# A new written-out order for the first 28 steps of a fused windowed-attention and feed-forward kernel

## The chip, the cores and the metric

The kernel runs on one core of a Trainium2 chip. The metric is device time in microseconds (us) for one execution. A run of the kernel before is given as the median of three. One further execution was profiled, and every trace number comes from that one.

## What is computed

The reference has two parts. The first is attention over 8 batches, 8 heads, 576 tokens and a head size of 64. A query sees at most 32 keys: in the first four heads the 32 latest tokens, in the other four every fourth token of the latest 128. The second part is a feed-forward network on the 4608 tokens with 512 columns, over 2048 hidden columns.

```
scores = scale * q @ k.T;  scores = where(mask, scores, -1e9)
attn   = exp(scores - max(scores));  attn = attn / (sum(attn) + 1e-9)
x      = attn @ v                      # reshaped to 4608 x 512
h      = x @ w_in
out    = (h * clip(h + 3, 0, 6) / 6) @ w_out
```

## The kernel before

**Tiles.** Attention is cut into 48 pieces, called trios here after the name in the code; a trio is 192 token rows of four heads. Tokens for the feed-forward part are cut into 12 chunks of 384, hidden columns into 16 blocks of 128. The matmuls of the feed-forward part keep full precision by three products: high part by high part, low by high, high by low. So each x and each weight is split into two tiles first.

**Steps.** A step is one chunk by one block of hidden columns: a first product G (12 matmuls, L486 to L488), a ReLU on ScalarE (L494), a gate on VectorE (L497), a split into two parts (ScalarE L501, VectorE L505), and a second product H (9 matmuls, L536 to L538). Chunks 0 and 1 take turns in the first 32 steps. The first chunk needs trios 0 to 4, the second trios 2 to 9.

**The written order.** The first 28 steps, the first 12 trios, the split of all weights and all their loads are ordered by hand in one string, `ORDER`, of 588 names. Each engine keeps the order in which its own names stand there. TensorE, ScalarE, VectorE and the load queue of SyncE (SP) are all issued in that order and each works strictly from front to back. The letters of a name say what it is:

| Name | Engine | What it does (lines) |
|---|---|---|
| k, v, w, M | SP | load of a trio's queries and keys (L174), of its values (L183), of a half block of weights (L424), of a part of the mask (L670) |
| B, V | TensorE | scores of a trio, interleaved with the values product of an earlier trio when `FOLLOW` names one (L279, L203, L213); V is a values product alone |
| R, S, X | VectorE, VectorE, ScalarE | row maximum (L240), subtraction (L244), exponential (L250) |
| E, CA | TensorE, ScalarE | three transposes of the exponentials (L296), copy to SBUF (L309) |
| Z, Y, CX | VectorE, TensorE, ScalarE | normalisation (L255, L256, L258), three transposes (L296), copy (L313) |
| XH, XL | ScalarE, VectorE | the two parts of x (L387, L393) |
| U, Q, s, j, a, h, l | ScalarE and VectorE | split of a half block of weights: L439, L443 on ScalarE, L447, L453, L460 on VectorE, L463 on ScalarE, L469 on VectorE |
| G, RE, T, GH, GL, H | see Steps | one step; the number counts steps |

A name such as `w0@R1` puts a wait on top: the load w0 is issued only when R1 is done, and every later load stands behind it on SP. Below, names of this table are used.

```
for name in ORDER.split():
    name, _, behind = name.partition("@")
    kind = name.rstrip("0123456789")
    issued[name] = first_operations[kind](int(name[len(kind) :]))
    if behind:
        tc.add_manual_dep(issued[name].ins, issued[behind].ins.name, ...)
```

**Limits besides the order.** In the built program each load also waits until the load eight places before it has landed, so at most eight are under way. There are two PSUM banks for G, so a G starts only when the gate of the G two before it is done. What TensorE runs is fed to it as a stream of instructions, one weight load and one matmul for each of its matmuls; a paired block B has 97 of each, E and Y three, G 12, H 9.

**After the string** a planner in the kernel (`_in_time`, L1000) orders the other 36 steps, the other 36 trios and a second scheme for chunks 4 to 11. Its input is the same for both versions, because both strings hold the same names.

Of the kernel before, what the change touches and what calls it, by code (L numbers as in the profile page):

```python
# [45 lines left out]
ORDER = """
k0 M0 M1 k2 k1 v0 k3 v2 B0 v1 k5 R0 S0 X0 E0 B1 CA0 B2 R1 S1 w0@R1 X1 Z0 E1 k4@X1 R2 CA1 Y0 v4@CA1 B3 S2 CX0 XH0
k6@S2 X2 XL0 v6@XL0 v3@XL0 Q0 U0 E2 s0 Z1 CA2 B4 R3 j0 S3 w2@j0 a0 X3 v5@a0 h0 Y1 Z2 B6 CX1 XH1 R4 Y2 R6 E3 CX2 XL1
CA3 S6 XH2 B5 S4 X6 w4@XH2 XL2 X4 Q2 l0 E6 U2 Z3 E4 k7@E6 CA6 R5 CA4 Y3 v7@CA6 s2 V4 CX3 S5 k8@CX3 XH3 j2 X5 XL3
v8@j2 Q4 E5 Z4 U4 w13@E5 CA5 a2 Y4 B7 s4 CX4 w6@a2 j4 h2 XH4 l2 k9@j4 B8 Z5 k10@l2 R7 Y5 XL4 w7@R7 CX5 Z6 G0 Q13 XH5  # L50
S7 w1@Q13 Q6 R8 X7 XL5 Y6 U6 S8 E7 G1 CX6 a4 CA7 s6 XH6 j6 X8 h4 XL6 B9 w5@G1 RE0 a6 RE1 l4 h6 k11@RE1 T0 E8 Q7 Z7
G2 CA8 GH0 R9 Q1 v9@GH0 GL0 U1 S9 U7 Y7 T1 B10 X9 s1 CX7 l6 GH1 v10@CX7 j1 XH7 E9 G3 R10 RE2 CA9 XL7 Q5 S10 U5 Z8
B11 X10 RE3 a1 GL1 h1 E10 T2 Y8 CA10 Z9 CX8 V10 GH2 R11 XH8 Y9 l1 CX9 Z10 H0 XH9 XL8 XL9 w3@XL8 S11 Y10 G8 GL2 CX10
w16@S11 T3 X11 s5 XH10 s7 GH3 XL10 E11 RE8 GL3 G6 CA11 j5 U3 w28@CA11 T8 Q3 a5 GH8 G10 j7 RE6 w11@GH8 h5 GL8 U16 T6
l5 Q16 G4 s16 GH6 a7 RE10 Q28 j16 v11@a7 h7 T10 H2 w8@j16 Q11 a16 U28 l7 h16 s3 H3 s28 GH10 GL6 l16 RE4 j3 Q8
w30@RE4 V11 U8 T4 GL10 GH4 G20 w17@U8 Z11 GL4 w9@Z11 a3 Y11 s8 RE20 G13 j28 CX11 h3 T20 XH11 j8 Q30 H4 XL11 U30 l3
w29@Q30 GH20 a8 Q17 a28 U17 H1 GL20 RE13 s17 h8 T13 Q9 j17 GH13 H8 U9 l8 w31@GH20 h28 GL13 Q31 a17 U31 G12 s9 l28
h17 Q29 j9 U29 l17 w14@GL20 G25 Q14 a9 RE12 s31 h9 s30 T12 U14 H20 l9 RE25 s14 GH12 T25 GL12 G5 w15@T25 j14 GH25 j31
GL25 a14 H13 RE5 a31 h14 T5 Q15 l14 U15 H12 j30 GH5 h31 s15 GL5 j15 G18 l31 w23@j14 Q23 a15 a30 h15 G11 s29 RE18 l15
h30 T18 l30 w18@U15 GH18 H10 j29 RE11 GL18 T11 a29 Q18 G27 GH11 U18 GL11 h29 s18 H18 l29 w19@T18 Q19 RE27 j18 U19  # L60
T27 a18 GH27 H25 s19 h18 GL27 l18 w10@Q18 Q10 U10 j19 H11 U11 s10 a19 s11 h19 j10 G22 l19 w12@a19 j11 a10 G15 RE22
a11 h10 T22 h11 l10 GH22 H6 l11 w20@j10 Q12 RE15 GL22 Q20 T15 U20 G14 GH15 s20 U12 GL15 j20 U13 s12 H22 RE14 a20 T14
h20 s13 GH14 l20 w21@l11 G7 Q21 GL14 U21 j13 j12 G24 a13 RE7 a12 h13 T7 h12 l13 w22@l20 H14 GH7 RE24 l12 GL7 T24 G17
s21 Q22 j21 GH24 U22 GL24 a21 U23 G16 RE17 s22 s23 h21 T17 j22 GH17 G9 l21 w24@l12 Q24 a22 U24 j23 h22 H24 s24 l22
j24 w25@l22 a23 H15 RE16 GL17 h23 a24 RE9 T16 h24 l23 G26 GH16 T9 Q25 GL16 U25 l24 w27@GH16 GH9 s25 G19 j25 a25 H17
h25 Q27 l25 H16 RE26 GL9 w26@H17 k12 k13 v12 v13 M2 RE19 T26 T19 G21 GH26 GH19 Q26 H9 U26 s26 U27 j26 H7
RE21 GL26 a26 T21 h26 GL19 H5 GH21 l26 GL21 s27 j27 G23 a27 h27 H21 l27 RE23 T23 GH23 H19 GL23 H23
"""


# [1126 lines left out]
```

## Time and profile before

| | us |
|---|---|
| median of 3 runs | 863.64 |
| lowest and highest | 863.01, 863.70 |
| the profiled execution, its own time | 864.73 |
| span of the trace in that execution | 863.0 |
| TensorE busy in the span | 848.5 |
| VectorE busy, ScalarE busy | 563.0, 496.3 |

The span starts with the first instruction of the program; 1.73 us of the profiled execution lie outside it. In a row of the trace, a number of us or ns is followed by engine, line, operation, the tile that is written and the tiles that are read. "Idle before" is time in which the engine stood still just before such an instruction, with what ended it. "issue" as the cause means that the engine waited for nothing that the profile shows as a semaphore or a transfer.

### The profile page before, as it was taken

The page shows a single profiled execution, that of the slowest core. Times are in us where ns is not written, and L with a number is a line of the kernel's source. Part 1 is how long each engine was busy: PE and PEld are TensorE (multiplying, and loading weights), DVE is VectorE, ACT ScalarE, POOL GpSimd, SP SyncE. Part 2 cuts the span into 40 slices and gives each one's busy share as a digit, 9 for nine tenths or more (in the row PEclk, how much of TensorE's full clock was granted, in tenths as well). Part 3 has the DMA queues.
Part 4 walks back from the last instruction along what each step waited for, and adds up shares of the span by engine and source line. Part 5 has one row for each costly group of instructions (what it writes and reads, how often), then busy time and mean ns, then how long its engine had stood idle before and what let it go on. Part 6 is the DMA issues. An engine that isn't in the chain of part 4 may idle for free.

```text
span 863.0 us, 20520 instructions
## 1 busy us (share of the span) xinstructions
PE 848.5 (98%) x8540; PEld 756.6 (88%) x8540; DVE 563.0 (65%) x1148; ACT 496.3 (58%) x1034; POOL 31.3 (4%) x78
## 2 busy tenths in 40 slices
PE   7799999999999999999999999999999999999998
PEld 5588999899899999898898888888888889999997
DVE  4799996668887887655667665567566466343332
ACT  3688775357766657665556646545754545543334
POOL 0000000001201000100000000000000000000000
PEclk7799999999999999999999999999999999999999
DMA  8747433565583583654444646443735422853001
GB/s 285 267 147 240 123 117 118 179 205 183 184 256 130 189 286 112 243 171 159 137 137 150 246 153 208 138 136 122 273 113 152 155 80 92 301 177 107 1 1 73
DMA packets 69420, 141.18 MB, mean 164 GB/s; under 512 B 5200, under 2 KB 19536, under 8 KB 69328
## 3 DMA queue, kind: packets, MB, share of 16 engines
q1 hardware_dynamic: 69328, 139.88, 48.2%
q8 instruction: 67, 1.10, 0.5%
q14 instruction: 25, 0.20, 0.1%
HBM read 115.74 MB, written 24.12 MB: 162 GB/s over the span
## 4 chain that ended last, share of the span: by engine, by line
PE 96%; DVE 2%; issue 1%; ACT 0%; DMA 0%; SPq 0%
PE ps_o L646 11%; PE ps_o L648 10%; PE ps_o L647 10%; PE ps_x L656 9%; PE ps_x L658 9%; PE ps_x L657 9%; PE ps_h L486 5%; PE ps_h L487 5%; PE ps_h L488 5%; PE ps_o L536 5%; PE ps_o L538 5%; PE ps_o L537 5%; PE ps_b L221 2%; PE ps_a L203 1%; PE ps_a L221 1%; PE ps_b L203 1%
## 5 line engine op out<-in xcount | busy, mean ns | idle before, releaser
L646 PE MATMUL ps_o<-wo,gh 128*128 128x512 f32 x384 | 151.9, 396 | 0.0
L648 PE MATMUL ps_o<-wo,gl 128*128 128x512 f32 x384 | 150.2, 391 | 0.0
L647 PE MATMUL ps_o<-wo,gh 128*128 128x512 f32 x384 | 150.1, 391 | 0.0
L656 PE MATMUL ps_x<-xh,ring 128*128 128x384 f32 x384 | 129.5, 337 | 0.0
L657 PE MATMUL ps_x<-xl,ring 128*128 128x384 f32 x384 | 129.0, 336 | 0.0
L658 PE MATMUL ps_x<-xh,ring 128*128 128x384 f32 x384 | 129.0, 336 | 0.0
L911 ACT COPY s<-ps_x 128x384 f32<-128x384 f32 x96 | 45.8, 477 | 135.2 <-PE ps_x L658 132.4
L917 DVE TENSOR_TENSOR s<-ps_x,s 128x384 f32<-128x384 f32 x96 | 53.2, 555 | 100.9 <-ACT s L911 54.0
L875 DVE TENSOR_TENSOR gl<-t,gh 128x384 fp32r<-128x384 f32 x128 | 71.2, 557 | 54.4 <-ACT gh L871 51.8
L871 ACT CAST gh<-t 128x384 fp32r<-128x384 f32 x128 | 65.6, 514 | 47.5 <-DVE t L879 46.8
L486 PE MATMUL ps_h<-xh,wi 128*128 128x384 f32 x256 | 88.4, 345 | 0.0
L487 PE MATMUL ps_h<-xl,wi 128*128 128x384 f32 x256 | 86.4, 338 | 0.0
L488 PE MATMUL ps_h<-xh,wi 128*128 128x384 f32 x256 | 86.4, 338 | 0.0
L648 PEld LDWEIGHTS ps_o<-wo,gl 128*128 128x128 f32 x384 | 72.1, 188 | 15.6
L646 PEld LDWEIGHTS ps_o<-wo,gh 128*128 128x128 f32 x384 | 72.1, 188 | 11.7
L647 PEld LDWEIGHTS ps_o<-wo,gh 128*128 128x128 f32 x384 | 72.1, 188 | 10.0
L879 DVE SCALAR_TENSOR_TENSOR t<-t,s 128x384 f32<-128x384 f32 x96 | 53.9, 562 | 40.5 <-ACT t L867 39.0
L867 ACT ACTIVATE t<-s,three 128x384 f32<-128x384 f32 x96 | 59.2, 617 | 28.8 <-DVE s L917 28.0
L656 PEld LDWEIGHTS ps_x<-xh,ring 128*128 128x128 f32 x384 | 72.2, 188 | 3.9
L657 PEld LDWEIGHTS ps_x<-xl,ring 128*128 128x128 f32 x384 | 72.2, 188 | 3.9
L536 PE MATMUL ps_o<-wo,gh 128*128 128x512 f32 x192 | 74.9, 390 | 0.0
L538 PE MATMUL ps_o<-wo,gl 128*128 128x512 f32 x192 | 74.7, 389 | 0.0
(98 smaller groups left out, 1569.1 us busy)
## 6 DMA issues: line engine op xcount, KB each, us to landing
ring<-sums SPq DMA_DIRECT2D x112, 512.0 KB, 6.0
st<-in_w SPq DMA_DIRECT2D x32, 512.0 KB, 4.0
kq<-in_qk SPq DMA_DIRECT2D x39, 416.0 KB, 4.2
v<-in_v SPq DMA_DIRECT2D x39, 390.0 KB, 5.3
out<-o SPq DMA_DIRECT2D x36, 256.0 KB, 2.2
sums<-wi SPq DMA_DIRECT2D x24, 256.0 KB, 7.2
sums<-sh SPq DMA_DIRECT2D x8, 512.0 KB, 3.3
sums<-v SPq DMA_DIRECT2D x8, 512.0 KB, 4.1
```

What stands on the lines that cost most here:

```text
L486: nc.tensor.matmul(ph, lhsT=wt(f, 0)[:, ks], rhs=a, start=(kt == 0), stop=False)
L487: nc.tensor.matmul(ph, lhsT=wt(f, 0)[:, ks], rhs=b, start=False, stop=False)
L488: ins = nc.tensor.matmul(ph, lhsT=wt(f, 1)[:, ks], rhs=a, start=False, stop=(kt == NK - 1))
L536: nc.tensor.matmul(po[c][tt], lhsT=gh[:, rows], rhs=wt(f, 2), start=first, stop=False)
L538: return nc.tensor.matmul(po[c][tt], lhsT=gl[:, rows], rhs=wt(f, 2), start=False, stop=(f == NF - 1))
L646: nc.tensor.matmul(bank, lhsT=gh[:, rows], rhs=wt(f, 2), start=first, stop=False)
L647: nc.tensor.matmul(bank, lhsT=gh[:, rows], rhs=wt(f, 3), start=False, stop=False)
L648: nc.tensor.matmul(bank, lhsT=gl[:, rows], rhs=wt(f, 2), start=False, stop=final)
L656: nc.tensor.matmul(bank, lhsT=tile_[:, 0, ks], rhs=h[:, kt], start=(start and kt == 0), stop=False, skip_group_check=True)
L657: nc.tensor.matmul(bank, lhsT=tile_[:, 0, ks], rhs=l[:, kt], start=False, stop=False, skip_group_check=True)
L658: nc.tensor.matmul(bank, lhsT=tile_[:, 1, ks], rhs=h[:, kt], start=False, stop=(kt == 1), skip_group_check=True)
L875: nc.vector.tensor_tensor(out=two[1], in0=t[0], in1=two[0].bitcast(F32), op=ALU.subtract)
```

## The change

`ORDER` is replaced by another arrangement of the same 588 names, with other waits behind `@`. It was found by a search over a model of the engines that also has the fetching of instructions in it. Nothing else changes. The new string takes one line less, so line numbers after it are lower by one in the new kernel (L296 becomes L295).

```diff
 ORDER = """
-k0 M0 M1 k2 k1 v0 k3 v2 B0 v1 k5 R0 S0 X0 E0 B1 CA0 B2 R1 S1 w0@R1 X1 Z0 E1 k4@X1 R2 CA1 Y0 v4@CA1 B3 S2 CX0 XH0
...
+k0 M0 B0 k6 k1 R0 M1 S0 B6 v0 R6 X0 E0 S6 B1 CA0 k2 w2@B0 R1 B2 v1 U2 S1 X1 s2 Q2 X6 k3 E1 E6 CA1 B3 j2 a2 R2 S2 w0 U0
...
```

On TensorE, ahead of the first G, the names stood so and stand so now:

```
before: B0 E0 B1 B2 E1 Y0 B3 E2 B4 Y1 B6 Y2 E3 B5 E6 E4 Y3 V4 E5 Y4 B7 B8 Y5 | G0 Y6 E7 G1 B9 E8 G2
now:    B0 B6 E0 B1 B2 E1 E6 B3 E2 Y0 B4 E3 Y1 Y2 B5 B8 E5 E4 Y3 B7 V4 E8 Y6 E7 Y4 Y5 B9 | G1 Y7 B10 E9 G2
```

**Place 1, the head of TensorE's order.** Before: the mask product and the 24 score matmuls of B0, three transposes E0, then B1 and the start of B2.

```order
17 L279 LDWEIGHTS mi
18 L279 MATMUL ps_a<-mi 128x384
19 L203 MATMUL ps_a<-first 32x64 x24
20 L296 MATMUL ps_a<-ident,e 128x128 x3
21 L279 LDWEIGHTS mi
22 L279 MATMUL ps_a<-mi 128x384
23 L203 MATMUL ps_a<-first 32x64 x24
```

Now, at the same place:

```order
17 L278 LDWEIGHTS mi
18 L278 MATMUL ps_a<-mi 128x384
19 L202 MATMUL ps_a<-first 32x64 x24
20 L278 LDWEIGHTS mi
21 L278 MATMUL ps_a<-mi 128x384
22 L202 MATMUL ps_a<-first 32x64 x24
23 L295 MATMUL ps_a<-ident,e 128x128 x3
```

The block B6 has moved between B0 and the transposes E0.

**Place 2, TensorE just ahead of the first G.** Before: the last two matmuls of the paired block B8, the transposes Y5, and G0.

```order
336 L213 MATMUL ps_a<-first,a 32x65
337 L203 MATMUL ps_a<-first 32x64
338 L296 MATMUL ps_a<-ident,x 128x128 x3
339 L486 MATMUL ps_h<-xh,wi 128x384
340 L487 MATMUL ps_h<-xl,wi 128x384
```

Now: the values product V4, the transposes E8, Y6, E7, Y4 and Y5, and the start of the block B9, whose 48 small matmuls come ahead of the first G (G1).

```order
334 L212 MATMUL ps_a<-first,a 32x65 x24
335 L295 MATMUL ps_a<-ident,e 128x128 x3
336 L295 MATMUL ps_a<-ident,x 128x128 x3
337 L295 MATMUL ps_a<-ident,e 128x128 x3
338 L295 MATMUL ps_a<-ident,x 128x128 x6
339 L278 LDWEIGHTS mi
340 L278 MATMUL ps_a<-mi 128x384
341 L212 MATMUL ps_a<-first,a 32x65
```

The first G has moved behind one more paired block and three more groups of transposes; B5 and B8 now follow each other without anything between, and B7 follows after three groups of transposes.

**Place 3, the head of VectorE's order.** Before: R0, S0, R1, S1, Z0, R2.

```order
2 L240 TENSOR_REDUCE mx<-ps_a 128x6
3 L244 TENSOR_TENSOR e<-ps_a,mx 128x384
4 L240 TENSOR_REDUCE mx<-ps_a 128x6
5 L244 TENSOR_TENSOR e<-ps_a,mx 128x384
6 L255 TENSOR_SCALAR z<-ps_a 128x6
7 L256 RECIPROCAL z<-z 128x6
8 L258 TENSOR_TENSOR x<-ps_a,z 128x384
9 L240 TENSOR_REDUCE mx<-ps_a 128x6
```

Now: R0, S0, R6, S6, R1, S1, then three operations of the split of weight half block 2, then R2.

```order
4 L239 TENSOR_REDUCE mx<-ps_a 128x6
5 L243 TENSOR_TENSOR e<-ps_a,mx 128x384
6 L239 TENSOR_REDUCE mx<-ps_a 128x6
7 L243 TENSOR_TENSOR e<-ps_a,mx 128x384
8 L446 TENSOR_SCALAR va<-va 128x512
9 L452 SCALAR_TENSOR_TENSOR va<-st,va 128x512
10 L459 ISA va<-va 128x1024
11 L239 TENSOR_REDUCE mx<-ps_a 128x6
```

The first weight work has moved ahead of R2 and Z0; before, VectorE's first weight operation stood behind XL0.

On SP, the loads ahead of the paired block B5 were k0 M0 M1 k2 k1 v0 k3 v2 v1 k5 w0 k4 v4 k6 v6 v3; they are now k0 M0 k6 k1 M1 v0 k2 w2 v1 k3 w0 k4 v2 w4 w6 v6 k5 v3. Four half blocks of weights stand among them instead of one.

More of the change, by code (lines that the diff above doesn't have):

```diff
@@ L46 @@
 ORDER = """
-k0 M0 M1 k2 k1 v0 k3 v2 B0 v1 k5 R0 S0 X0 E0 B1 CA0 B2 R1 S1 w0@R1 X1 Z0 E1 k4@X1 R2 CA1 Y0 v4@CA1 B3 S2 CX0 XH0
[L48 to L66, printed above, removed]
@@ L67 @@
-RE21 GL26 a26 T21 h26 GL19 H5 GH21 l26 GL21 s27 j27 G23 a27 h27 H21 l27 RE23 T23 GH23 H19 GL23 H23
+k0 M0 B0 k6 k1 R0 M1 S0 B6 v0 R6 X0 E0 S6 B1 CA0 k2 w2@B0 R1 B2 v1 U2 S1 X1 s2 Q2 X6 k3 E1 E6 CA1 B3 j2 a2 R2 S2 w0 U0
+Q0 k4@R0 X2 s0 v2 w4 j0 Z0 R3 E2 Z1 CA2 w6 S3 v6@X2 CA6 U4 U6 s4 Y0 X3 B4 a0 E3 Z2 s6 Y1 k5 j6 h2 Y2 CA3 v3@a2 R4 CX0
+CX1 k8@CA1 S4 B5 Q4 X4 XH0 j4 R5 Q6 B8 l2 S5 CX2 X5 Z3 XL0 E5 XH2 R8 Z6 k7 v5 v4@S3 E4 Y3 XH1 a6 S8 CA5 CA4 CX3 B7 XL1
+V4 k9@CA6 w28@S4 R7 S7 XH3 X8 X7 Z4 E8 Y6 v7@Q6 CX6 E7 CA7 w14 Z5 v8@E3 XL3 k10@Y3 Y4 CX4 Y5 XH4 B9 w16 w1@Z3 Q16 XL2
@@ new lines @@
+Q1 XL4 U16 w5 CA8 a4 h4 Z7 Q14 R9 G1 Y7 CX5 S9 h0 s16 j16 U14 CX7 B10 l4 s14 X9 Q5 U28 XH6 RE1 k11 R10 a16 E9 G2 Z8
+v9@XH3 CA9 h6 T1 XH5 XH7 w8@G2 l0 Y8 S10 B11 w7@CA9 l6 v10@E8 U5 XL6 X10 h16 RE2 CX8 j14 G3 Z9 Y9 XH8 T2 l16 RE3 XL5
+G0 CX9 E10 XH9 T3 RE0 G13 R11 s5 XL7 v11@E10 XL8 Q8 w15@X10 T0 U7 XL9 CA10 U1 RE13 w20@RE0 GH1 V10 S11 X11 a14 GH0 T13
+G10 s1 w18@l16 h14 w3@G0 j1 G4 U15 RE10 l14 a1 RE4 w12@E10 E11 T10 j5 GL0 T4 w17 a5 U8 U18 Z10 GH2 h1 l1 s7 h5 G8 G11
+s18 j7 CA11 H0 s8 RE11 T11 Q20 V11 Q7 Q3 G6 GH4 l5 Q18 GL1 j8 RE8 j18 Y10 GH10 U17 Q15 s15 U12 GL2 a7 U3 T8 Z11 a8 h7
@@ new lines @@
+a18 Q12 w29 j15 Q17 RE6 GL4 h18 H2 Y11 T6 G18 G20 s3 CX10 CX11 RE18 h8 s12 XH11 s28 l7 GL10 U29 Q29 H4 l8 RE20 j3
+w10@j18 U20 GH3 Q28 T18 j28 G12 H10 l18 w11@CX10 RE12 a3 s17 a28 GH8 a15 XH10 T12 s20 h28 GH18 G15 h3 T20 GL8 l28 U11
+G5 h15 H8 GL3 s29 j17 U10 l3 H1 j12 Q11 j29 XL10 RE5 a12 GH11 h12 GH13 T5 GL11 j20 a17 RE15 w22@GL3 s10 l15 G22 w9@H1
+H11 a20 s11 j10 h20 RE22 T15 h17 l20 G25 l12 Q10 H3 GL18 j11 RE25 w19@G22 a11 U9 a29 T25 U22 T22 s22 j22 h29 G9 a10
+Q22 a22 l29 l17 GL13 Q19 h10 G24 GH12 w24@H11 s9 GH25 GL25 RE9 l10 U19 H18 GH6 Q9 h22 H13 h11 j9 GL12 T9 RE24 G14 s19
@@ new lines @@
+a9 l11 GH15 GH5 w31 T24 h9 H25 j19 l22 w21 l9 G17 U24 U31 s31 GL5 s24 RE14 w26 Q24 a19 U21 T14 j31 s21 GL6 GH24 h19
+j21 Q31 l19 Q21 a21 H12 RE17 h21 G26 a31 h31 U26 T17 l21 w30 Q26 H5 RE26 j24 U30 a24 GH20 XL11 s26 l31 G7 GL15 GL24
+GH17 j26 H6 T26 GH22 s30 G16 H24 j30 h24 Q30 w13@XL11 a26 GL17 h26 H15 l24 GH9 U13 RE16 T16 l26 M2 Q13 RE7 s13 G19 a30
+GH26 h30 j13 a13 w23@T17 h13 H17 RE19 GH14 l30 GL20 l13 Q23 T19 GL14 U23 s23 w25@h31 G27 GL26 T7 w27 GH19 j23 a23 GH7
+GL19 RE27 h23 GH16 T27 H14 l23 U25 U27 GL7 GL16 G23 G21 RE23 RE21 H20 s25 Q25 s27 Q27 j25 GL9 j27 GL22 H9 T21 a25 h25
@@ L68 @@
+a27 H22 T23 GH23 H16 v12 k12@h25 GH21 GH27 h27 k13@s27 GL21 l25 l27 H21 GL23 H19 H23 H7 v13@GH7 GL27
 """
```

## Prediction, made before the changed kernel ran

> **What bounds the kernel now.** I read the table by stages first. Its columns are busy us (and instructions) of each engine, the granted TensorE clock, the DMA share and the rate.
>
> ```profile
> 0.00:10.00 10.00, 6.49 (x97) 3.32 (x101) 1.50 (x3) 2.28 (x3) 0.59 (x6) 0.87 0.81 287
> 10.00:20.00 10.00, 9.04 (x301) 6.64 (x296) 5.80 (x14) 4.01 (x8) 0.00 (x0) 0.61 0.88 287
> 20.00:30.00 10.00, 7.71 (x252) 5.64 (x241) 9.79 (x26) 8.86 (x20) 0.00 (x0) 1.00 0.84 264
> 30.00:40.00 10.00, 6.39 (x201) 5.17 (x202) 5.69 (x14) 2.46 (x7) 0.00 (x0) 0.57 0.88 332
> 50.00:58.00 8.00, 7.76 (x266) 6.62 (x266) 7.79 (x20) 7.24 (x18) 0.00 (x0) 1.00 0.41 126
> 58.00:160.00 102.00, 102.00 (x568) 92.92 (x567) 89.42 (x173) 71.50 (x136) 0.00 (x0) 1.00 0.51 164
> 160.00:863.00 703.00, 699.13 (x6742) 627.01 (x6740) 434.42 (x885) 390.46 (x827) 30.68 (x72) 1.00 0.46 157
> ```
>
> From 58 us on TensorE never stands still until the last stage, where 3.9 us are missing. The new order ends near 160 us. So all there is to win or lose lies in the first 58 us, and a shift of TensorE there is carried to the end. Second, the groups of TensorE's instructions between 4.8 and 58 us, for the idle time in the last column:
>
> ```profile
> L213 PE MATMUL ps_a<-first,a 64*32 64x65 f32 x432 | 15.5, 260 | 0.7 <-ACT a L309 0.7
> L203 PE MATMUL ps_a<-first 64*32 64x64 f32 x432 | 14.0, 269 | 3.4 <-issue 3.4
> L296 PE MATMUL ps_a<-ident,e 128*128 128x128 f32 x33 | 6.5, 315 | 2.6 <-ACT e L250 2.6
> L296 PE MATMUL ps_a<-ident,x 128*128 128x128 f32 x29 | 5.8, 314 | 2.1 <-DVE x L258 2.1
> ```
>
> That is 8.8 us of idle, 3.4 of them inside blocks and with no semaphore behind them. Besides, the granted clock was 0.61 from 10 to 20 us and 0.57 from 30 to 40. Third, TensorE in order of time around the largest gap:
>
> ```profile
> 15.04 0.50 PE L279 MATMUL ps_a<-mi 32*128 32x384 bf16 x1
> ...
> 19.59 0.21 PE L203 MATMUL ps_a<-first 64*32 64x64 f32 x1 [0.32 <-issue]
> ...
> 27.29 1.25 PE L213 MATMUL ps_a<-first,a 64*32 64x65 f32 x48
> ...
> 33.11 0.50 PE L279 MATMUL ps_a<-mi 32*128 32x384 bf16 x1
> ...
> 37.05 0.31 PE L203 MATMUL ps_a<-first 64*32 64x64 f32 x1 [3.10 <-issue]
> ```
>
> B8 starts at 33.11, does four matmuls, and goes on at 37.05. What it waited for shows in the DMA queues, first from 26 to 34.5 us, then from 34.5 to 37.1 us:
>
> ```profile
> DMA packets 860, 2.70 MB, mean 318 GB/s; under 512 B 92, under 2 KB 92, under 8 KB 859
> q1 hardware_dynamic: 859, 2.70, 92.7%
> ...
> DMA packets 311, 1.03 MB, mean 394 GB/s; under 512 B 31, under 2 KB 31, under 8 KB 310
> q1 hardware_dynamic: 310, 1.01, 99.6%
> q8 instruction: 1, 0.02, 2.3%
> ```
>
> An instruction packet came only after 34.5 us, then the block went on. The page counts them for the whole span (packets, MB, share):
>
> ```profile
> PE 848.5 (98%) x8540; PEld 756.6 (88%) x8540; DVE 563.0 (65%) x1148; ACT 496.3 (58%) x1034; POOL 31.3 (4%) x78
> q8 instruction: 67, 1.10, 0.5%
> ```
>
> 17,080 instructions by 67 packets are 255 to a packet, so it is TensorE's stream, 256 at a time. Counted in matmuls and loads, the gaps at 19.59 and 37.05 lie three packets apart. If a packet is asked for when the packet before the running one is used up, TensorE has 256 instructions to live on. Going back 256 from 37.05 leads through 8 of B8, 194 of B7 and 12 of Y4 and E5 (with some semaphore instructions) into V4, at about 28.0 us; back from 19.59 it leads to about 15.5 us, early in B3. So the turnaround, from asking to use, was 4.1 us once and 9.0 us once. The two refills between them were no slower than TensorE's own 256 instructions, since there is no third gap "issue" in the group above.
>
> **The change, part by part.** Prices on TensorE, from starts at full clock: a paired block, B9 to E8; a group of transposes, Y6 to E7; a G, up to the next step's H; G0 in the kernel before, up to Y6.
>
> ```profile
> 45.55 0.33 PE L279 MATMUL ps_a<-mi 32*128 32x384 bf16 x1
> ...
> 47.14 0.33 PE L296 MATMUL ps_a<-ident,e 128*128 128x128 f32 x1
> ...
> 163.34 0.34 PE L486 MATMUL ps_h<-xh,wi 128*128 128x384 f32 x1
> ...
> 165.43 0.39 PE L536 MATMUL ps_o<-wo,gh 128*128 128x512 f32 x1
> ...
> 39.56 0.67 PE L486 MATMUL ps_h<-xh,wi 128*128 128x384 f32 x1
> ...
> 42.70 0.49 PE L296 MATMUL ps_a<-ident,x 128*128 128x128 f32 x3
> 43.02 0.49 PE L296 MATMUL ps_a<-ident,e 128*128 128x128 f32 x3
> ```
>
> These are 1.59, 0.32 and 2.09 us; V4 is half a block, 0.8. The measure of the change is where TensorE stands when its first G starts: 39.56 us before.
>
> *Head (places 1 and 3).* B6, R6 and S6 fill time in which TensorE waited for X0. That time does not reach the first G by itself, because loads set the pace next.
>
> *Loads up to B5.* They now hold seven k, five v, four w and two parts of the mask (KB of each load behind its count):
>
> ```profile
> st<-in_w SPq DMA_DIRECT2D x32, 512.0 KB, 4.0
> kq<-in_qk SPq DMA_DIRECT2D x39, 416.0 KB, 4.2
> v<-in_v SPq DMA_DIRECT2D x39, 390.0 KB, 5.3
> ...
> mi<-in_mask SPq DMA_DIRECT2D x1, 160.0 KB, 3.6
> mi<-in_mask SPq DMA_DIRECT2D x1, 24.0 KB, 3.4
> ```
>
> 7 x 416 + 5 x 390 + 4 x 512 + 184 KB are 7.26 MB. The critical chain has the mask's first part landing after
>
> ```profile
> 1.18 3.61 DMA mi<-in_mask
> ```
>
> at 4.79 us, with k0 some 0.59 MB. The other 6.67 MB take 16.9 us at 394 GB/s and 21.0 at 318, so B5 can start at 21.7 to 25.8 us. SP now lets eight loads run where it held them back before (w0 waited for R1), so I take 22.5, near the fast end.
>
> *Instruction packets from B5 on (place 2).* The boundaries keep their counts: 11 instructions into B5, 69 into B8, 110 into B7, 43 into B9, 72 into B10. Without waits TensorE needs between them 2.1 us; 2.9 (rest of B8, three groups of transposes, part of B7); 3.5; and 4.2 (rest of B9, G1, Y7, part of B10). The first three are below the shorter turnaround of 4.1 us, so here the packets set the pace. I take 4.6, a little above the shorter, because the load queue is full all this time. Then the boundaries fall at 22.6, 27.2, 31.8 and 36.4 us, and G1 starts 1.24 us later (151 instructions of B9), at 37.6. At the next boundary, in B10, TensorE waits 0.4 us more.
>
> *VectorE up to G1.* XL4 must be done. V4 ends at 31.8 + 0.7 + 0.8 = 33.3 us, and behind it stand Z4, Z5, XL3, XL2, XL4. Prices from these starts (Z5, R7, XL4 of the kernel before):
>
> ```profile
> 33.21 0.16 DVE L255 TENSOR_SCALAR z<-ps_a 128x6 f32<-128x6 f32 x1 [0.43 <-PE ps_a L213]
> ...
> 34.11 0.55 DVE L240 TENSOR_REDUCE mx<-ps_a 128x6 f32<-128x384 f32 x1
> 34.57 0.90 DVE L393 TENSOR_TENSOR xl<-xf,xh 128x96 fp32r<-128x96 f32 x2
> ```
>
> 2 x 0.90 + 3 x 0.87 are 4.4 us, so XL4 ends at 37.7 us, and that is when G1 starts; ScalarE's copies for XL4 fall between and are shorter.
>
> *What stands behind.* After G1 the order alternates G with B10, B11, transposes and waits on a half block each. Walking VectorE's names at the same prices, I find G1 to G13 each ready within some tenths; I put 0.2 us for all. Weights now begin to be split ahead of R2, and VectorE had 12.6 of 102 us free from 58 to 160 us, so TensorE coming earlier by some us has cover there; if that cover were gone, the gain would be given back there and no more.
>
> *The sum.* G1 at 37.7 + 0.4 + 0.2 = 38.3 us, against G0 at 39.56: 1.3 us. By then B9 (1.59) and E7, E8, Y6 (0.96) have also been done that were still to come: 2.5 us. Together 3.8 us. Not counted is that G0 took 3.14 us at the low clock instead of 2.09: the pauses for packets will hold the clock down in the new order too, or else 1.05 us more are won. The profiled execution took 864.73 us, so 860.9 in it; it lay 1.09 above the median of 863.64, so the forecast is 859.8 us. About 0.2% (1.7 us) is what a measurement of this kernel can tell from no change.
>
> [...]
>
> **The rivals.**
>
> *Hidden packets.* The packets come so early that they never set the pace. For it: between the two gaps, two came in time in the same full queue. Against it: three boundaries now lie closer together than 4.1 us. B5 at 21.7, then 1.59 + 1.59 + 0.96 + 1.59 + 0.8 to the end of V4, then 4.4 for VectorE give G1 at 32.6 us: 7.0 + 2.5 = 9.5 us, less 0.2, is 854.3. Chance 0.13. [...]
>
> *One long packet.* One of the three has the long turnaround, 9.0 in place of 4.6: 4.4 us later, 864.2, no change. Chance 0.12. For it: of four refills, one was that long.
>
> *Slower: the load queue starves the stream.* SP's deeper queue makes the long turnaround the rule between B5 and B9. Two of three long give 868.6, all three 873.0. It decides from a mean of 6.4 us (4.6 + (3.8 + 1.7) / 3). For it: the long one fell at a share of 0.88 and a rate that the new order holds from the start. Against it: the 4.1 us fell at the same share. Chance 0.10.
>
> *Nothing gained in the end.* TensorE comes earlier, but between 58 and 160 us a half block of weights is late, and the gain is lost again: 863.6. Chance 0.04; the 12.6 us free on VectorE speak against it.
>
> **How the numbers follow.** The forecast, 0.61, is a gain of 1 to 6 us; some 0.03 of it lie below 1.7 us. Faster: 0.58 + 0.13 = 0.71. Same: 0.03 + 0.12 + 0.04 = 0.19. Slower 0.10. The range goes from 854.8, near the hidden packets, to 864.2, one long packet; it leaves out the slower rival and the lower part of the hidden one.
>
> **What would show it.** Right: gaps "issue" of 1 to 2 us in B8 and B7, a smaller one in B9, no other TensorE gap over 1 us from B5 to H0, the first G at 37 to 39 us, behind B9, and 102 of 102 us busy after 58. Hidden packets: no gap "issue", and G1 before 34. Wrong: a gap "issue" over 4 us, G1 after 42, a TensorE gap that ends with a transfer of weights, or idle time of TensorE between 60 and 160 us.

## The result and the profile after

| | before | new order |
|---|---|---|
| median of 6 runs, in turns on one chip | 863.49 us | 866.90 us |
| lowest and highest | 863.00, 864.94 | 866.13, 868.01 |
| the profiled execution, its own time | 864.73 | 866.13 |
| span of its trace | 863.0 | 864.4 |

The new order takes 1.0039 times the time of before (95% interval 1.0026 to 1.0052): it is slower by 3.4 us. In one of the runs further down (e15), one execution of twelve took 1045 us at a granted clock of 0.75, and the median given for e15 is that of the other eleven. The two traces differ by 1.4 us only. The profiled execution of before lay 1.2 us above its median, that of the new order is the fastest of its six and 0.8 below; 1.4 + 1.2 + 0.8 are the 3.4. So the traces show some 40% of the loss, and the rest has to be looked for in what differs from one execution to the next.

The table by stage of the new order, with the columns of the one shown of before:

```profile
0.00:10.00 10.00, 7.52 (x158) 3.77 (x158) 2.61 (x5) 2.28 (x3) 0.59 (x6) 1.00 0.81 278
10.00:20.00 10.00, 4.68 (x212) 3.58 (x200) 5.89 (x12) 4.15 (x8) 0.00 (x0) 0.95 1.00 373
20.00:30.00 10.00, 8.64 (x247) 6.84 (x245) 8.43 (x21) 7.02 (x15) 0.00 (x0) 0.71 0.96 328
30.00:40.00 10.00, 7.01 (x224) 6.20 (x225) 6.13 (x17) 4.41 (x12) 0.00 (x0) 0.83 0.94 324
...
50.00:58.00 8.00, 8.00 (x138) 7.46 (x137) 7.93 (x18) 7.19 (x17) 0.00 (x0) 1.00 0.54 183
58.00:160.00 102.00, 101.80 (x608) 92.20 (x607) 90.86 (x177) 70.20 (x135) 0.00 (x0) 1.00 0.42 139
160.00:863.00 703.00, 700.52 (x6747) 628.16 (x6745) 431.83 (x880) 390.54 (x827) 30.81 (x72) 1.00 0.47 158
```

TensorE begins earlier (7.52 us busy in the first ten, 6.49 before), and then loses more than half of the stretch from 10 to 20 us, with the transfer engines fully busy (share 1.00). From 50 us on it hardly stands still until the last stage (0.2 us between 58 and 160). The same groups of TensorE's instructions between 4.8 and 58 us tell by what:

```profile
L212 PE MATMUL ps_a<-first,a 64*32 64x65 f32 x432 | 14.8, 247 | 3.5 <-issue 3.3 <-ACT a L308 0.2
L202 PE MATMUL ps_a<-first 64*32 64x64 f32 x432 | 12.5, 237 | 7.6 <-issue 7.3 <-DMA first<-in_qk 0.2
L295 PE MATMUL ps_a<-ident,e 128*128 128x128 f32 x33 | 6.5, 324 | 0.9 <-POOL ident L672 0.9
...
L295 PE MATMUL ps_a<-ident,x 128*128 128x128 f32 x30 | 5.8, 319 | 0.1
```

The waits for ScalarE's `e` and VectorE's `x` that before had (2.6 and 2.1 us) are gone, as the order meant them to be. "issue" grew from 3.4 to 10.6 us: all 5.3 us of idle time between 10 and 20 us are of this kind. Where these waits lie, in order of time, with the starts of B3, B5, B9 and G1 among them:

```profile
13.04 0.21 PE L202 MATMUL ps_a<-first 64*32 64x64 f32 x1 [1.71 <-issue]
...
14.29 0.33 PE L278 MATMUL ps_a<-mi 32*128 32x384 bf16 x1
...
19.54 0.31 PE L202 MATMUL ps_a<-first 64*32 64x64 f32 x1 [3.61 <-issue]
...
26.03 0.33 PE L278 MATMUL ps_a<-mi 32*128 32x384 bf16 x1
...
30.66 0.24 PE L202 MATMUL ps_a<-first 64*32 64x64 f32 x1 [2.01 <-issue]
...
36.26 0.31 PE L212 MATMUL ps_a<-first,a 64*32 64x65 f32 x1 [2.13 <-issue]
...
41.13 0.33 PE L278 MATMUL ps_a<-mi 32*128 32x384 bf16 x1
...
43.00 0.21 PE L212 MATMUL ps_a<-first,a 64*32 64x65 f32 x1 [1.16 <-issue]
...
44.01 0.44 PE L485 MATMUL ps_h<-xh,wi 128*128 128x384 f32 x1
```

They stand in B2, B3, B8, B7 and B9, each time inside a block and 256 instructions of TensorE, or 512, behind the one before. So in the new order five of the first six packets of instructions come late. The DMA queues from 13.1 to 17 us, and then from 17 to 17.4, show the second of them:

```profile
DMA packets 499, 1.60 MB, mean 409 GB/s; under 512 B 55, under 2 KB 55, under 8 KB 499
q1 hardware_dynamic: 499, 1.60, 102.9%
...
DMA packets 46, 0.18 MB, mean 440 GB/s; under 512 B 6, under 2 KB 6, under 8 KB 45
q1 hardware_dynamic: 45, 0.16, 100.2%
q8 instruction: 1, 0.02, 16.1%
```

TensorE took up the packet before at 13.04 us, which by the prediction's reading is when the next is asked for. 499 packets of loads passed first; the instruction packet started after 17.0, and its first instruction ran at 19.54.

### The profile page after: what moved, and what is told of

It is laid out like the page before. It is cut to its first block, busy times and chain, and to the rows that moved or that the text cites. A ratio compares the mean times of both kernels' runs of the same rounds, so it can differ in the third digit from the quotient of the medians.

```text
span 864.4 us, 20503 instructions
## 1 busy us (share of the span) xinstructions
PE 846.9 (98%) x8540; PEld 755.6 (87%) x8540; DVE 562.8 (65%) x1148; ACT 495.6 (57%) x1034; POOL 31.4 (4%) x78
## 4 chain that ended last, share of the span: by engine, by line
PE 97%; issue 1%; DMA 1%; SPq 0%; DVE 0%; ACT 0%; POOL 0%; POOLq 0%
PE ps_o L645 11%; PE ps_o L647 10%; PE ps_o L646 10%; PE ps_x L655 9%; PE ps_x L657 9%; PE ps_x L656 9%; PE ps_h L485 5%; PE ps_h L486 5%; PE ps_h L487 5%; PE ps_o L537 5%; PE ps_o L535 5%; PE ps_o L536 5%; PE ps_b L220 2%; PE ps_a L212 1%; PE ps_a L202 1%
## 5 line engine op out<-in xcount | busy, mean ns | idle before, releaser
L645 PE MATMUL ps_o<-wo,gh 128*128 128x512 f32 x384 | 152.0, 396 | 0.0
L646 PE MATMUL ps_o<-wo,gh 128*128 128x512 f32 x384 | 150.0, 391 | 0.0
L493 ACT ACTIVATE t<-ps_h,three 128x384 f32<-128x384 f32 x64 | 37.2, 582 | 71.6 <-PE ps_h L487 62.1
```

Source lines behind the costliest of these rows:

```text
L645: nc.tensor.matmul(bank, lhsT=gh[:, rows], rhs=wt(f, 2), start=first, stop=False)
L646: nc.tensor.matmul(bank, lhsT=gh[:, rows], rhs=wt(f, 3), start=False, stop=False)
```

## The experiments

Three theories stood at the outset. *Queue*: an instruction packet waits longer the more loads are under way when it is asked for, and the new order keeps more of them under way (5.5 in the mean of its first six packets, 3.3 in before). *Block*: the packet's time is what it is, and blocks that stand closer no longer hide it. *Load*: the early halves of weights make keys and values late, and packet waits only fill that time.

All runs in one table. "Issue" is the sum of TensorE's waits called issue before 60 us. "Ask to start" is the mean over the head's first six packets, from the moment TensorE takes up the packet before (found by counting its instructions in the trace) to the start of the packet's record in the instruction queue. That the packet is asked for at this moment is the prediction's reading; no trace records the asking. From start to first use it was 2.2 to 3.0 us, mostly 2.4, for each packet that was waited for. The ratio is that to the kernel before, on the same chip.

| run | what it is | first G | issue | ask to start | ratio [95%] |
|---|---|---|---|---|---|
| | before | 39.6 | 3.4 | 2.6 | 1 |
| | new order | 44.0 | 10.6 | 3.6 | 1.0039 [1.0026, 1.0052] |
| e7 | new order again | 44.5 | 8.5 | 3.4 | 1.0047 [1.0029, 1.0064] |
| e1 | new, at most 3 loads under way | 43.1 | 0.9 | 1.8 | 1.0115 [1.0095, 1.0135] |
| e2 | new, 2 | 47.1 | 1.0 | 1.4 | 1.0233 [1.0212, 1.0253] |
| e11 | new, 5 | 45.2 | 7.9 | 3.1 | 1.0052 [1.0039, 1.0065] |
| e3 | before, 3 | 38.7 | 0.0 | 1.4 | 1.0019 [1.0004, 1.0033] |
| e4 | before, loads not held | 38.7 | 2.9 | 2.8 | 1.0019 [1.0008, 1.0031] |
| e5 | new, 3 half blocks later | 44.1 | 10.5 | 3.5 | 1.0086 [1.0061, 1.0110] |
| e6 | the same, 4 under way | 43.1 | 4.1 | 2.3 | 1.0112 [1.0087, 1.0136] |
| e12 | new, B6 put back | 44.8 | 5.7 | 3.0 | 1.0048 [1.0033, 1.0063] |
| e8 | new, 100 instructions more | 46.2 | 9.0 | | 1.0309 [1.0276, 1.0342] |
| e10 | before, 100 more | 41.4 | 5.6 | | 1.0316 [1.0287, 1.0345] |
| e9 | new, 256 more | 45.7 | 10.1 | | 1.0061 [1.0040, 1.0083] |
| e13 | new, half the matmuls | 35.2 | 0.0 | | 0.9993 [0.9981, 1.0005] |
| e14 | before, half the matmuls | 36.9 | 0.0 | | 0.9968 [0.9954, 0.9982] |
| e15 | new, half as many, twice as wide | 36.6 | 0.0 | | 1.0004 [0.9991, 1.0017] |
| e16 | before, half as many, twice as wide | 35.2 | 0.0 | | 1.0007 [0.9992, 1.0023] |

### Fewer loads under way (e1 to e4)

From the eighth load on, each also waits for the landing of the one three (e1, e3) or two (e2) places before:

```diff
+            if kind in "kvwM":
+                under_way.append(name)
+                if 7 < len(under_way) <= 64:
+                    tc.add_manual_dep(
+                        issued[name].ins, issued[under_way[-1 - 3]].ins.name,
+                        mybir.DependencyInfo(mybir.DependencyClass.Sync, mybir.DependencyReason.DATA), reason="few under way",
+                    )
```

e4 is before without the written waits of its first 16 loads that have one:

```diff
-k0 M0 M1 k2 k1 v0 k3 v2 B0 v1 k5 R0 S0 X0 E0 B1 CA0 B2 R1 S1 w0@R1 X1 Z0 E1 k4@X1 R2 CA1 Y0 v4@CA1 B3 S2 CX0 XH0
...
+k0 M0 M1 k2 k1 v0 k3 v2 B0 v1 k5 R0 S0 X0 E0 B1 CA0 B2 R1 S1 w0 X1 Z0 E1 k4 R2 CA1 Y0 v4 B3 S2 CX0 XH0
...
```

> The new order, but from the eighth load on each load also waits until the load three places before it has landed, so at most three are under way instead of eight. Queue theory (the time from asking for an instruction packet to its use grows with the loads under way): the packets' mean turnaround falls from 6.0 us to 4.5 to 5, the sum of TensorE's gaps 'issue' over 1 us from 10.6 to 3 to 6 us, and the time to 861 to 864. Block theory (the turnaround does not depend on the loads, the waits come from blocks that stand closer together): gaps stay at 9 to 11 us, time 866 to 868. Load theory (the early weights make the keys and values late): loads land later still, TensorE waits for transfers, time over 868.

> The same with at most two loads under way. Queue theory: gaps 'issue' shrink further, to 1 to 4 us in sum, but the loads now come too slowly for the blocks and waits for transfers appear; 861 to 867, the gaps 'issue' decide. Block theory: gaps 'issue' stay at 9 to 11 us, and late loads add to that, over 867. Load theory: over 870.

> The kernel before, with at most three loads under way from the eighth load on. Queue theory: the gap of 3.1 us in B8 shrinks to 0 to 1.5 us, time 861 to 863. Block theory: the gap in B8 stays at 3 us, time 863.5. Load theory: loads get later, 863.5 or more.

> The kernel before without the written waits of its first 16 loads of keys, values and weights that have one, so that they are issued as early as the limit of eight lets them. Queue theory: the gap in B8 stays or grows and new gaps 'issue' of 1 to 4 us come up in B2, B3 and B4, in sum 6 to 10 us instead of 3.4; time 865 to 869. Block theory: gaps as before, time 863 to 864. Load theory: loads land earlier, time 861 to 863.

TensorE's waits up to 60 us in e1 (us in total, times, longest):

```profile
PE ps_a L295 <- ACT e L249: 7.4, 6, 1.8
PE ps_a L212 <- ACT a L308: 2.9, 1, 2.9
...
PE ps_a L202 <- issue: 0.9, 1, 0.9
```

The mechanism of the queue theory holds: with fewer loads under way the packets start 1.8 and 1.4 us after they are asked for instead of 3.6, in the same packed order of blocks, and the waits called issue all but vanish. The block theory, which has that time fixed, is out. But the time, which the queue theory had at 861 to 864 us for e1, got worse: 872.15, and 882.42 in e2. The wait for packets turned into a wait for ScalarE, on which an exponent now stands behind conversions of early weights whose loads come later: ScalarE itself waited 12.2 us for weights before 60 us in e1, 2.6 in the new order. In before (e3) the same step took the 3.4 us of issue away and gained nothing either.

e4 is a miss for the queue theory, which had 6 to 10 us of issue and 865 to 869 us there: it came to 2.9 us and 864.16. Its first three packets were asked for with eight loads under way and took 2.9 to 3.7 us to start, much as in the new order, but TensorE needed longer for the 256 instructions in between, and of these three only the second was waited for noticeably (1.7 us). So slow packets were mostly covered there by TensorE's own work.

Eight is the limit, not what runs all the time. When the first six packets of the new order were asked for, 7, 7, 6, 4, 4 and 5 loads were under way. Over the 66 packets of the eleven runs that have a value in the column, the mean from ask to start was 1.5 us with two loads under way, 1.8 with three, 2.9 with four, 3.1 with five and 3.7 with six to eight, with a wide spread in each group (1.1 to 6.7 us with four).

### The same again (e7)

> The new order unchanged, on the chip of this call, for a second profile and more times. All theories: 865 to 868 us and a ratio of 1.002 to 1.006 to the kernel before; the waits called issue sum to 9 to 13 us below 60 us of the span in this profile too; from one execution to another their sizes may differ by 1 to 2 us, their places not, since the stream has the same number of instructions.

867.24 us, with the same six places and other sizes: 0.45, 2.56, 0.87, 1.74, 2.12 and 0.75 us, 8.5 in sum, a little below the 9 to 13 that were expected, where the first trace has 1.71, 3.61, none, 2.01, 2.13 and 1.16. Single packet waits differ by 1 us and more from one execution to the next; that may be how executions of one kernel come to differ, but the times of executions without a trace can't be taken apart.

### Three half blocks of weights later (e5, e6)

The loads of w4, w0, w6 stand behind k9, their conversions behind X7 and XL4; e6 also has at most four loads under way.

```diff
...
-CX1 k8@CA1 S4 B5 Q4 X4 XH0 j4 R5 Q6 B8 l2 S5 CX2 X5 Z3 XL0 E5 XH2 R8 Z6 k7 v5 v4@S3 E4 Y3 XH1 a6 S8 CA5 CA4 CX3 B7 XL1
-V4 k9@CA6 w28@S4 R7 S7 XH3 X8 X7 Z4 E8 Y6 v7@Q6 CX6 E7 CA7 w14 Z5 v8@E3 XL3 k10@Y3 Y4 CX4 Y5 XH4 B9 w16 w1@Z3 Q16 XL2
-Q1 XL4 U16 w5 CA8 a4 h4 Z7 Q14 R9 G1 Y7 CX5 S9 h0 s16 j16 U14 CX7 B10 l4 s14 X9 Q5 U28 XH6 RE1 k11 R10 a16 E9 G2 Z8
...
+XH0 R5 B8 l2 S5 CX2 X5 Z3 XL0 E5 XH2 R8 Z6 k7 v5 v4@S3 E4 Y3 XH1 S8 CA5 CA4 CX3 B7 XL1 V4 k9@CA6 w4 w0 w6
+w28@S4 R7 S7 XH3 X8 X7 U4 Q4 Z4 E8 Y6 v7@S4 CX6 E7 CA7 w14 Z5 v8@E3 XL3 k10@Y3 Y4 CX4 Y5 XH4 B9 w16 w1@Z3 Q16
+XL2 Q1 XL4 s4 j4 U0 Q0 s0 j0 a0 U6 Q6 s6 j6 a6 U16 w5 CA8 a4 h4 Z7 Q14 R9 G1 Y7 CX5 S9 h0 s16 j16 U14 CX7 B10
...
```

> The new order with three of its four early half blocks of weights (0, 4 and 6: 1.5 MB) loaded only behind key 9, and their five conversions each moved to stand behind the exponent X7 and the token part XL4; otherwise the new order. Queue theory (packets of TensorE's instructions wait longer the more loads are under way): fewer bytes stand ahead of the packets asked for in B2 and B3, whose waits of 1.7 and 3.6 us become under 1 and under 2 us, the waits called issue sum to 5 to 8 instead of 10.6 us, B5 starts at 22 to 24 us instead of 26.0, the first G at 39 to 42 instead of 44.0, time 861 to 864.5. Block theory (the turnaround is what it is, only the blocks stand closer): the waits called issue keep a sum of 9 to 11.5, first G 43 to 45, time 865 to 868. Load theory (late keys and values set the pace and the packet waits lie inside that): B5 starts 2 us or more earlier whatever the packet waits do, and the time falls under 864.5 with an issue sum still over 9.

> The same as the run with three half blocks of weights loaded later, and besides each load from the eighth on waits until the load four before it has landed, so that at most four are under way. Queue theory: from ask to start a packet takes about 2 us (1.8 with three under way, 3.6 with eight), the waits called issue sum to 0.5 to 3 us, ScalarE no longer stands behind early weight conversions as in the run of the new order with three under way (7.4 us there), first G at 38 to 41, time 859 to 863. Block theory: issue sum 8 or more, 865 to 868. Load theory: fewer under way only makes the loads later, so new waits for ScalarE and transfers of 4 us or more take the place, 865 to 870.

TensorE's waits up to 60 us in e5:

```profile
PE ps_a L204 <- issue: 7.2, 3, 3.9
PE ps_a L214 <- issue: 3.3, 2, 1.7
PE ps_a L297 <- DVE x L259: 1.7, 1, 1.7
```

A miss for the queue theory in its wording about bytes. The waits of B2 and B3 went from 5.3 to 3.3 us, as it said, but the later ones grew, the sum stayed at 10.5 and the first G at 44.1. The load theory missed as well. The loads under way are only spread differently: 7, 3, 4, 8, 6 and 5 of them when the six packets were asked for, few in B2 and B3 where the waits shrank and more behind, and in the mean a packet still starts 3.5 us after it is asked for. In e6 ask to start came down to 2.3 us and issue to 4.1, and 6.0 us of waits for VectorE's `x` and 3.8 for loads took the place, in kind what the load theory said of e6; the time was 872.47 us. So the early weights are not the culprit by themselves, and moving them costs more than it brings.

### Five under way, and B6 back in its place (e11, e12)

e11 has the lines of e1 with 5 for 3. In e12, B6 stands behind B4 and R6, S6, X6, E6, CA6 with it; its first two lines:

```diff
-k0 M0 B0 k6 k1 R0 M1 S0 B6 v0 R6 X0 E0 S6 B1 CA0 k2 w2@B0 R1 B2 v1 U2 S1 X1 s2 Q2 X6 k3 E1 E6 CA1 B3 j2 a2 R2 S2 w0 U0
-Q0 k4@R0 X2 s0 v2 w4 j0 Z0 R3 E2 Z1 CA2 w6 S3 v6@X2 CA6 U4 U6 s4 Y0 X3 B4 a0 E3 Z2 s6 Y1 k5 j6 h2 Y2 CA3 v3@a2 R4 CX0
+k0 M0 B0 k6 k1 R0 M1 S0 v0 X0 E0 B1 CA0 k2 w2@B0 R1 B2 v1 U2 S1 X1 s2 Q2 k3 E1 CA1 B3 j2 a2 R2 S2 w0 U0 Q0
+k4@R0 X2 s0 v2 w4 j0 Z0 R3 E2 Z1 CA2 w6 S3 v6@X2 U4 U6 s4 Y0 X3 B4 B6 a0 E3 Z2 s6 Y1 k5 j6 h2 Y2 CA3 v3@a2 R4
...
```

> The new order in which each load from the eighth on also waits for the landing of the load five before it, so at most five are under way. Queue theory: a packet takes 2.2 to 3.0 us from ask to start, between the 1.8 with three and the 3.6 with eight under way; the waits called issue sum to 3 to 7 us; ScalarE's waits for early weights that it brings (7.4 us with three) stay under 4; first G 41 to 44, time 864 to 870. Rival (a packet's wait depends on the bytes that the transfer engines carry, not on how many loads are under way): ask to start stays over 3.2 us, since the transfer engines stay busy, and the issue sum over 8.

> The new order with piece 6 put back to about its place before: B6 behind B4 instead of behind B0, its R6, S6, X6, E6 and CA6 with it; loads and early weights stay. Packing theory (blocks that stand closer ask for packets faster than they come): 52 fewer matmuls stand between B0 and B3, so the waits in B2 and B3 (1.7 and 3.6 us) shrink to under 3 us together, first G at 40 to 43, time 862 to 866. Chain theory (each packet is asked for when the one before it is taken up, so the head up to the first G is a chain of six turnarounds of 5 to 6 us whatever stands in it, as long as the loads are under way): the wait moves to the later blocks, first G stays at 43 to 46 and the time at 865 to 869.

e11 came out between its two theories (3.1 us, issue 7.9, first G 45.2) and tells nothing of whether loads or bytes count. e12 is clearer. TensorE's waits up to 60 us:

```profile
PE ps_a L214 <- issue: 4.1, 3, 2.7
PE ps_a L297 <- POOL ident L674: 2.2, 1, 2.2
PE ps_a L204 <- issue: 1.6, 1, 1.6
```

Issue in B2 and B3 shrank to 1.2 us, as the packing theory said; the first G stayed at 44.8 and the time at 867.05, as the chain theory said. That fits a chain in which each packet is asked for when the one before is taken up, so that a wait that is avoided early comes back at a later packet.

### Where the packets end (e8, e10, e9)

Small warm-up matmuls on zeros shift TensorE's stream: by 100 instructions in e8 and e10, by 256, one whole packet by the prediction's count, in e9 (136 in place of 4 + 54; the lines are those of e8).

```diff
-    for _ in range(WARM):
-        nc.tensor.matmul(idle, lhsT=zeros[:, :P], rhs=zeros[:, P : P + 512], start=True, stop=True)
+    for i in range(4 + 54):
+        n = 512 if i < 4 else 32
+        nc.tensor.matmul(idle[:, :n], lhsT=zeros[:, :P], rhs=zeros[:, P : P + n], start=True, stop=True)
```

> The new order with another warm-up: 4 matmuls of 512 columns and 54 of 32 columns instead of 8 of 512, so 100 more instructions (a weight load and a matmul each) stand ahead of B0. The products are of zeros in both. All theories in which the waits called issue are waits for packets of 256 instructions: the places of the waits move 50 matmuls back in the stream (the first wait that stood within B2 now stands near the end of B1 or at the start of B2, and each later one 50 matmuls earlier too), their sum stays within 7 to 13 us, time within 2.5 us of the new order. Rival (the waits belong to the blocks, or to data that they read): each wait stays at the same matmul of the same block.

> The kernel before with the warm-up of 4 matmuls of 512 columns and 54 of 32 columns, 100 more instructions ahead of B0. Packet theory: the stretch from 160 us on has the same instructions in both kernels and the packets end at the same places in it, so it gets the same waits as the shifted new order: 12 to 20 us of idle time called issue between 190 and 400 us and a time of 880 to 892. Rival (the new order carried something into the later stretch): at most 3 us more than before, 862 to 867.

> The new order with 136 warm-up matmuls of 32 columns instead of 8 of 512 (products of zeros in both): 256 more instructions ahead of B0, one whole packet, so that every later packet ends at the same matmul as in the new order. Packet theory: the waits from 160 us on, which came with 100 more instructions (16.7 us of idle time and half clock), are gone again, idle time from 160 us on within 1 us of the new order's 2.5 us at its end; the waits called issue in the head stand at the same matmuls as in the new order; time 863 to 870. Rival (the other warm-up itself does it, by the clock or by the bank that it holds): the waits from 160 us on come again and the time is over 880.

891.02, 890.30 and 867.89 us. In e8 the head's waits are three (2.30, 3.19, 3.56 us), at the same counts of the stream and so 50 matmuls earlier in the work. That speaks against a rival by which they belong to blocks or their data. The 24 us more in e8, where the packet theory had it within 2.5 us of the new order, were lost elsewhere: TensorE's waits from 160 us on, in e8 and then in e10, where the new order, before and e9 have none:

```profile
PE ps_a L203 <- issue: 8.5, 4, 3.0
PE ps_a L221 <- issue: 8.2, 3, 4.6
```

```profile
PE ps_a L222 <- issue: 8.5, 3, 4.9
PE ps_a L204 <- issue: 8.4, 4, 2.9
```

Seven waits between 193 and 342 us (16.7 us in e8, 16.9 in e10), in front of the same seven matmuls in both, and gone with a shift of 256 (e9). So by these runs the waits called issue are waits for packets, and whether this packed stretch pays them hangs on where in it the packets end.

### Fewer packets (e13 to e16)

What stayed open is whether the packets hold the first G or only fill time. In the blocks of the first 12 pieces half of the matmuls are left out and the others take 64 columns of weights instead of 32. In e15 and e16 they also stream twice the columns, so that TensorE's work stays; the mask is then overwritten instead of added to. In all four the products of these pieces are not the reference's. 3 wide and 69 small warm-up matmuls keep the packets' ends in the later stretch.

```diff
-            ps[at : at + QB, 2 * QB * i : 2 * QB * (i + 1)],
-            lhsT=x[rows, KW + QB * n : KW + QB * (n + 1)], rhs=x[rows, QB * kb : QB * (kb + 2)],
+            ps[at : at + m, 2 * QB * i : 2 * QB * i + 2 * m],
+            lhsT=x[rows, KW + QB * n : KW + QB * n + m], rhs=x[rows, QB * kb : QB * kb + 2 * m],
...
-            if ts is not None:
+            if ts is not None and not (u and ts < NFIRST):
```

> The new order with half the matmuls in the blocks of the first 12 pieces: each takes 64 columns of weights for two products of 32, and its partner is left out (the products of 12 pieces are not the reference's; data, sizes, loads and all other instructions stay). 64 small warm-up matmuls stand ahead of B0, so that TensorE has four packets (1024 instructions) less up to the end of the order and packets end at the same places after it. Packet theory: no wait called issue over 1 us but perhaps one, the first G at 36 to 39.5 us instead of 44.0, time 858 to 862.5, and 2 us or more under the kernel before with the same halving: the gain that was predicted (3.8) comes back. Rival (loads, VectorE or ScalarE hold the first G anyway): the first G stays at 41.5 to 44.5, TensorE's idle time is then ended by semaphores of DMA, DVE or ACT, time 864 to 868, no faster than the halved kernel before by more than 1 us.

> The kernel before with the same halving of the matmuls of the first 12 pieces and the same 64 small warm-up matmuls (the products of 12 pieces are not the reference's). Packet theory: the one wait called issue (3.4 us at 37 us) goes, the waits for ACT and DVE stay, the first G at 37 to 39 instead of 39.6, time 861 to 864, over the halved new order by 2 us or more. Rival: time 861 to 864 and within 1 us of the halved new order or under it.

> The new order with half the matmuls in the blocks of the first 12 pieces, each of 64 columns of weights and twice the columns streamed (128 or 130 instead of 64 or 65), the same small warm-up matmuls as in the halved runs (the products of 12 pieces are not the reference's, and the mask is not added in them). TensorE's streaming stays what it was, its packets become fewer. Packet theory: waits called issue under 1 us in sum, the first G at 36 to 39 us (44.0 with all packets, 35.2 with half the matmuls), time 859.5 to 862.5 and at least 1 us under the widened kernel before. Rival 1 (the lighter TensorE did it): the first G at 40 us or later, time over 864. Rival 2 (behind the first G, TensorE waits for VectorE and ScalarE whatever the packets do, as in the halved run with its 2.4 us at 42.5): first G at 36 to 39, but 1.5 us or more of idle time on semaphores between the first G and 58 us, and no gain over the widened kernel before.

> The kernel before with the same half as many, twice as wide matmuls and the same warm-up (the products of 12 pieces are not the reference's, and the mask is not added in them). Packet theory: the one wait called issue (3.4 us) goes, the first G at 36.5 to 38.5 us instead of 39.6, time 861 to 863, over the widened new order by 1 us or more. Rivals 1 and 2: time 859.5 to 863, level with the widened new order or under it.

861.76, 860.13, 862.98 and 863.02 us. The halved pair has its first G at 35.2 and 36.9 us, and the new order is still 1.6 us behind where the packet theory had it 2 us or more ahead, but there TensorE's own work is less too; the widened pair is the cleaner one. The first G of e15 and then of e16 (line numbers are higher by two):

```profile
36.56 0.44 PE L487 MATMUL ps_h<-xh,wi 128*128 128x384 f32 x1
```

```profile
35.16 0.42 PE L488 MATMUL ps_h<-xh,wi 128*128 128x384 f32 x1
```

TensorE streams as much as before in e15 (216 matmuls of 275 ns where there were 432 of 237 and 247):

```profile
L214 PE MATMUL ps_a<-first,a 64*64 64x130 f32 x216 | 14.2, 275 | 1.4 <-ACT a L310 0.7 <-DMA first<-in_v 0.7
L204 PE MATMUL ps_a<-first 64*64 64x128 f32 x216 | 14.1, 275 | 0.0
```

Its waits up to 58 us:

```profile
PE ps_a L297 <- ACT e L251: 3.8, 7, 1.3
PE idle L146 <- DVE zeros L142: 1.3, 1, 1.3
PE ps_a L297 <- DVE x L259: 0.9, 2, 0.6
```

With fewer packets the first G of the new order comes 7.4 us earlier (44.0 to 36.6), with the same loads and the same work on all other engines: the packets held it, and rival 1 falls. What the low clock has in this is not told apart: with the packet waits its 10.2 us in the new order went too. The new order falls from 866.9 to 863.0 us, or from 1.0039 to 1.0004 of before. The kernel before falls not at all (863.0, or 1.0007), although its first G comes 4.4 us earlier; a widened paired block takes it 1.80 us (B9, 41.11 to 42.91) instead of 1.59, which gives part of that back. In the traces, the first G behind the order starts at 163.34 us in before, 164.45 in the new order, 160.89 in e16 and 160.11 in e15: 1.1 us behind with all packets, 0.8 ahead with fewer. The times do not show these 0.8 us, and their intervals (some 1.3 us to each side) could hide them. So the whole loss of the new order goes with its packets. The other half of the packet theory fails: without packet waits the new order is level with before as far as the times tell, and not 3.8 us ahead. Its first G is 1.4 us later than that of e16, with 2.5 us more work done ahead of it. In place of the packet waits stand seven waits for an exponent `e`, 3.8 us. That is rival 2 only in part: six of them, 2.5 us, lie ahead of the first G, and behind it stands one of 1.3 us, where rival 2 had 1.5 or more.

## Why the prediction was wrong

The result lies 2.7 us above the upper end of the range.

**The step that failed** is in *Head*: "That time does not reach the first G by itself, because loads set the pace next", with packets counted "from B5 on". B6, B1, B2 and B3 ran early as foreseen, and so used up the packets early; by the prediction's reading the first three were asked for at about 7, 13.0 and 19.5 us, with loads under way all that time. The waits in B2 and B3, 1.71 + 3.61 us, were in no term. B5 started at 26.03 us, not 22.5, and directly behind Y2: from 19.54 on TensorE had run without a gap, at the low clock for most of it (0.51 from 19.0 to 25.9), so neither the loads nor a semaphore held it. The last load that B5 needs, v3, landed at 24.33. Where the packets were out of the way (e15), the loads did set the pace, and near the forecast: B5 started at 22.21 and stood 0.71 us for v3:

```profile
23.25 0.29 PE L214 MATMUL ps_a<-first,a 64*64 64x130 f32 x1 [0.71 <-DMA first<-in_v]
```

**Packets from B5 on.** The places were right: 2.01 us in B8, 2.13 in B7, 1.16 in B9, no other gap over 1 us up to H0. The size was too small. With the boundary in B5 at about 26.5 us by count, the turnarounds were 4.1 (26.5 to 30.66), 5.6 (to 36.26) and 6.7 (to 43.00), in place of 4.6 each: 2.7 us more. The wait of 0.4 us in B10 did not come.

**VectorE up to G1** was right to a tenth: V4 ended at 38.6, and 4.4 us later XL4 was done.

```profile
40.45 2.60 DVE L392 TENSOR_TENSOR xl<-xf,xh 128x192 fp32r<-128x192 f32 x6
```

It ended at 43.05, 1.0 us before the packets let G1 start; the forecast had the two within 0.1 us of each other (37.7 and 37.6). So VectorE, which the forecast had as the last thing G1 waits for, was not: the packets were.

**The first G** closes: the last boundary at 43.0 instead of 36.4 is 6.6, of which 3.9 stood already at the boundary in B5 (26.5 for 22.6) and 2.7 came behind it. G1 began 1.0 us after it: 44.01 instead of 37.7.

**What stands behind, and the sum** held to some tenths. 39.56 - 44.01 + 2.5 is -1.95 us. Of the 1.05 us of clock, not counted, 0.9 were won: G1 ran at full clock (1.00 from 44.01 to Y7 at 46.22). That leaves a loss of 1.0, and the first G behind the order came 1.1 us later; the profiled executions differ by 1.4 at their ends. TensorE was busy for 101.8 of 102 us after 58.

**The rivals.** "The load queue starves the stream" had the right sign and half the mechanism. It put all long turnarounds between B5 and B9, where their mean came to 5.5 us and not the 6.4 from which it decides; the larger part of the delay, 3.9 of 6.6 us, was made ahead of B5. "One long packet" did not happen either: the longest turnaround behind B5 was 6.7 us, not 9.0, and two of the three were longer than the 4.6 of the sum. "Hidden packets" is out, and e15 shows that even where they are hidden the first G comes at 36.6 and not at 32.6, with 2.5 us of waits for exponents ahead of it. "Nothing gained in the end" did not happen. The prediction's row with 859 data packets, shown for the wait in B8, starts too early: by the count of instructions the packet was asked for at 28.0 us, and from then to its start 710 data packets passed.

**What stays open.** Why a packet waits just 3.6 us with a limit of eight loads and 1.4 with a limit of two: whether it is the number of loads, their bytes or where in the queue the packet stands was not told apart (e5, e11). Loads are not all of it: in e4 a packet that by the reading above was asked for at 31.34 us started at 34.69, and the load queue moved nothing in between. TensorE stood at semaphores twice meanwhile (0.36 and 0.76 us); whether the packet is then asked for later, or held up by something else, no run shows. And which of VectorE's and ScalarE's early work makes the exponents late in e15; no run took that work out on its own.

## What to carry to other kernels

Here a stage ran many small matmuls while the load queue was full, the instruction queue had 67 packets for TensorE's 17,080 instructions, and the waits for them stood 256 or 512 instructions apart. Where the trace of another kernel shows the same, count TensorE's instructions from the first one on, mark every 256th, and treat the packets as a chain, in which each seems to be asked for when the last is taken up. Closing a gap ahead of one only moved the wait to the next here: in e12 issue in B2 and B3 fell from 5.3 to 1.2 us, and the first G came at 44.8 us instead of 44.0. A wait that was removed on the engine in front was a gain only as far as that chain and the load queue allowed; an order that took 4 us of semaphore waits away got 7 us of packet waits for it. Before moving or adding TensorE's instructions, look where the packets end in every packed stretch behind: the shift by 100 instructions, a part of a packet, cost 24 us in e8.
